# A first DFT stage moved to four 64x64 tiles of TensorE, with the mirrored sum formed ahead of it and the even and odd parts behind it

## The chip, the cores and the metric

The kernel runs on one core of a Trainium2 chip. Its time is device time in microseconds (us): the median of the runs of one kernel. The engines are TensorE (PE, with PEld for its loads of weights), VectorE (DVE), ScalarE (ACT), GpSimd (POOL) and SyncE (SP, which here only issues DMAs). Each runs its own instructions in order and waits for the others by semaphores.

## The reference

For each of 8 batches, x is 3008 x 256 in fp32. The real part of its two-dimensional Fourier transform, taken as 24064 rows of 256, goes through a feed-forward layer with the gate h * cos(h):

```python
def _attn_ref(x):                       # x: (8, 3008, 256)
    X = np.fft.fft(x, axis=1)
    X = np.fft.fft(X, axis=2)
    return X.real.astype(np.float32)

def _moe_ref(x, w_in, w_out):           # w_in: 256 x 2048, w_out: 2048 x 256
    h = x @ w_in
    g = h * np.cos(h)
    return (g @ w_out).astype(np.float32)
```

## The kernel before

**The transform.** The sequence of 3008 is split as 47 x 64. A first stage is a DFT of length 47 over rows s2 (24 of its frequencies are kept, the others follow by symmetry), a second stage one of length 64 over s1, and the DFT over the 256 columns is folded into the weights of the first feed-forward product (WC and WS). Since x is real, row s1 is joined with its mirror 64 - s1, so that 32 indices i remain, in eight chunks of four; and column d is joined with its mirror 256 - d into an even part (sum) and an odd part (difference) of 128 columns.

For one batch b and chunk c the first stage before the change does this:
- `load_x(b, p)` loads two chunks (p = 0 to 3) into an `xp` tile, the rows of x and the rows of its mirror interleaved on 96 partitions. These DMAs are issued on SP.
- `fold(b, c, e)` (L247, on GpSimd for batches 2 to 8, on VectorE for the first) forms the even part (e = 0) and the odd part (e = 1) of a chunk, 96x508; the two end columns 0 and 128 are copied by ScalarE through the list `small`.
- `first_half(b, c)` (L275) multiplies each part with its matrix from L: two matmuls of 96 rows and 64 columns of the array and 512 moving columns, the even one into partitions 0 to 63 of a PSUM bank `pz`, the odd one into 64 to 127. For chunk 0, L272 takes the first 128 columns with matrices of their own.
- `keep_z` (L301) copies `pz` to an SBUF tile `zs` on ScalarE. Column 128 is treated apart: `take_middle` gathers it into `xm`, `middle` (L323) multiplies it into `pm`, ScalarE copies that to `zm` (L917), and `patch_z` puts it into `zs`.
- `store_z` sends `zs` to DRAM (`zd`), `load_z` brings it back turned, and `second_half` (L366) is the second stage, whose result `pq` is the input of the feed-forward layer.

**The main loop.** A batch has six groups of output columns (256, the first 225) and a group has 8 steps, so `per` = 48 steps a batch; a step t has two half steps, k = 2t and 2t + 1 (u = 0, 1). For half step k, `cur`, `prev` and `old` are the units k, k - 1 and k - 2, and `done` is the step whose second product is now made. PE's order in a half step is: `mm1(cur, 0)` (L550, with WC), then second-stage matmuls `mm2(done, ...)` (L641, three of the step's seven), then `mm1(cur, 1)` (L550, with WS), and in odd half steps one `mm2` more. Around it, for each unit: `seed` (L531, ACT) writes a bias into a PSUM bank H, `act_e` (L562), `dve_h` (L566, DVE), `act_round` (L578), `dve_frac` (L582), `act_sin` (L588), `dve_g` (L592), and once a step `sums` on GpSimd (L608, L614, L615), which forms the operands S of four of the seven `mm2` matmuls. `combine_m` (GpSimd), `take_m` (ACT and DVE), `store_out` (a transpose on DVE, L761, then stores on SP) close a group.

**Where the first stage stands in it.** While batch b - 1 runs through the loop, `transform(b)` lists what is done for batch b at the end of which of the 48 steps: loads at 0, 2, 4, 6; folds of pair p at 8p + 6, 7, 9, 10; the two first-stage calls of a pair in the half step u = 0 of step 8p + 12; stores at 8p + 12; the middle column at 11. The four H banks are used in turn, and `borrow` lends the next two of them to a pair: `pz` and, with k = 1, the bank of unit k - 2, whose last reader is `dve_g`. `seed` of the next unit takes the first lent bank, so it comes behind `keep_z`.

```python
        pair = None if u else pairs.pop(t, None)
        if pair:
            b, c = pair
            pz = [first_half(b, c, borrow("pz"))]
        if old:
            dve_g(old)
            ...
        if pair:
            pz.append(first_half(b, c + 1, borrow("pz", 1)))
```

The functions in full:

Of the kernel before, what the change touches and what calls it, by code (L numbers as in the profile page):

```python
# [33 lines left out]
def _consts():  # L34
# [21 lines left out]
    LO = stack(np.sin(th), np.cos(th), -np.sin(thm), -np.cos(thm))  # L56
    LE0 = stack(np.cos(th), z, z, np.cos(thh))
    LO0 = stack(np.sin(th), z, z, np.sin(thh))
    L = np.concatenate([LE, LO, LE0, LO0], axis=1)
    L = np.concatenate([L, np.zeros((128 - NX, 256))], axis=0)  # L60

# [3 lines left out]
    for jj in range(NJ):  # L65
        phi = 2.0 * np.pi * np.outer(i, 47 * k2 + jj) / SEQ
        blk = np.concatenate([np.cos(phi), np.sin(phi)], axis=0)
        blk[0] = 1.0
        blk[NI] = np.where(k2 % 2 == 0, 1.0, -1.0)
        blk = blk.reshape(2, 2, 16, 64)  # L70
        for half in range(2):
            for r in range(2):
                for e in range(2):
                    p = 64 * half + 32 * r + 16 * e
                    B[p : p + 16, jj, 64 * e : 64 * e + 64] = blk[r, half]
# [7 lines left out]
        L.astype(np.float32),  # L83
        B.reshape(128, NJ * 128).astype(np.float32),
# [30 lines left out]
def kernel(  # L115
# [9 lines left out]
    L_np, B_np, CS_np = _consts()  # L125
    L_dr = nc.inline_tensor(L_np, name="dft_L")
    ident_dr = nc.inline_tensor(np.eye(128, dtype=np.float32), name="ident")
# [18 lines left out]
    def load_x(b, p):  # L146
        if (b, p) not in xs:
            take_x(b, p)
# [16 lines left out]

    CS = [cpool.tile([128, 256], FP, tag=f"CS{i}", name=f"CS{i}") for i in range(2)]
# [6 lines left out]
    L = cpool.tile([128, 256], FP, tag="L", name="L")  # L173
# [65 lines left out]
    def fold(b, c, e):  # L239
        lo = IP * (c % 2)  # L240
        xv = xs[b, c // 2].rearrange("r (i d) -> r i d", d=ND)[0:NX, lo : lo + IP]
        if b == 0:
            xfs[b, c] = xf0[c % 2]
        elif e == 0:
            xfs[b, c] = spool.tile([128, 2 * IP * 128], FP, tag="xf", bufs=2, name="xf")
        fv = xfs[b, c].rearrange("r (e i d) -> r e i d", e=2, d=128)[0:NX]
        (nc.gpsimd if b else nc.vector).tensor_tensor(  # L247
# [5 lines left out]
        if e:  # L253
            ends = dict(out=fv[:, :, :, 0].rearrange("r e i -> r i e"), in_=xv[:, :, 0:129:128])
            if b:
                small.append(ends)
            else:
                nc.gpsimd.tensor_copy(**ends)
# [3 lines left out]
    def first_half(b, c, pz=None):  # L262

        rows = NX if b else 128
        fv = xfs.pop((b, c)).rearrange("r (e c) -> r e c", e=2)[0:rows]
        LE, LO, LE0, LO0 = (L[0:rows, 64 * q : 64 * q + 64] for q in range(4))
        pz = pz or psum("pz", "M")
# [15 lines left out]
        if b:  # L283
            return pz
        if a:
# [5 lines left out]
            lhsT=LE,  # L291
# [4 lines left out]
        keep_z(b, c, pz)  # L296

    def keep_z(b, c, pz):
        tag, n = ("zs", 4) if b or c < 4 else ("pq", 8)
        zs = spool.tile([128, 512], FP, tag=tag, bufs=n, name="zs")  # L300
        nc.scalar.copy(out=zs, in_=pz)  # L301
        zss[b, c] = zs

    def patch_z(b, c):
        small.append(
            dict(out=zss[b, c][64:128, 0:512:128], in_=zm[64:128, IP * c : IP * c + IP])
        )

    xm = cpool.tile([128, NI], FP, tag="xm", name="xm")
    zm = cpool.tile([128, NI], FP, tag="zm", name="zm")  # L310

    def take_middle(b, p):
        xv = xs[b, p].rearrange("r (i d) -> r i d", d=ND)[0:NX]
        small.append(dict(out=xm[0:NX, XP * p : XP * p + XP], in_=xv[:, :, 128]))

    def clear_middle():
        pm = borrow("pm", 1)[64:128, 0:NI]
# [3 lines left out]
    def middle(pm):  # L321
        for i0, i1, q in ((0, 1, 2), (1, NI, 0)):
            nc.tensor.matmul(  # L323
                pm[:, i0:i1],
                lhsT=L[0:NX, 64 * q : 64 * q + 64],
                rhs=xm[0:NX, i0:i1],
                start=False,
                stop=True,
                skip_group_check=True,
# [5 lines left out]
    def store_z(b, c, j0=0, j1=NJ, eng=nc.sync):  # L335
        half, q = divmod(c, NCH // 2)
        if q == 0 and j0 == 0:
            zds[b, half] = dpool.tile([32, 2 * NJ * 128], FP, tag="zd", bufs=4, name="zd")
        zd, zs = zds[b, half], zss[b, c]
        for e in range(2):  # L340
# [4 lines left out]
            )  # L345

# [57 lines left out]
    def transform(b):  # L404
# [5 lines left out]
        for p in range(4):  # L410
            at(2 * p, load_x, b, p)
            at(7 + p, take_middle, b, p)
            for k in range(4):
                at(8 * p + (6, 7, 9, 10)[k], fold, b, 2 * p + k // 2, k % 2)
            pairs[per * (b - 1) + 8 * p + 12] = b, 2 * p
            for c in (2 * p, 2 * p + 1):
                at(8 * p + 12, store_z, b, c)
        middles.add(per * (b - 1) + 11)
# [365 lines left out]
    def chunk(c):  # L784
        fold(0, c, 0)
        fold(0, c, 1)
# [5 lines left out]
    first_half(0, 0)  # L792
    chunk(2)
    first_half(0, 1)
# [3 lines left out]
    store_z(0, 0, 0, 4)  # L798
    store_z(0, 1, 0, 4)
    chunk(3)  # L800
    first_half(0, 2)
    chunk(4)
    first_half(0, 3)
    store_z(0, 2, 0, 4)
    store_z(0, 3, 0, 4)
    chunk(5)
    first_half(0, 4)
    chunk(6)
    first_half(0, 5)
    store_z(0, 4, 0, 4, nc.scalar)  # L810
    store_z(0, 5, 0, 4, nc.scalar)
    load_z(0, 0, 0, 4)
    chunk(7)
    first_half(0, 6)
    store_z(0, 6, 0, 4, nc.scalar)
    first_half(0, 7)
# [179 lines left out]
```

## Time and profile before

| | |
|---|---|
| median of 3 runs | 1945.69 us (1945.51 to 1946.28) |
| the profiled execution | 1945.75 us, span 1944.0 us |
| granted TensorE clock | 0.999 |
| busy: PE, ACT, DVE, POOL | 99%, 78%, 75%, 72% of the span |
| share of the 16 DMA engines | 19.2% for the queue q1 over the span, 7 tenths in the first fortieth |
| first-stage matmuls L275 | 256 records, 63.1 us busy |
| folds on POOL, L247 | 112 of 1264 ns |
| copies of pz on ACT, L301 | 64 of 576 ns |

A matmul in fp32 stands in the trace as two records. A record's duration contains its way through the array, so the distance from start to start is what counts. The span starts with the first instruction; the time of an execution has 1.75 us around it. A bracket behind a line of the timeline tells how long the engine was idle before it and what ended that; for PEld this is not idle time of PE, which may still be streaming.

### The profile page before, as it was taken

What the parts mean: (1) busy time and instruction counts of PE and PEld (TensorE: products, weight loads), DVE (VectorE), ACT (ScalarE), POOL (GpSimd) and SP (SyncE); (2) the same over time, 40 slices, a digit from 0 to 9 for tenths busy, and PEclk for the clock granted to TensorE, in tenths of its full rate; (3) what the DMA queues carried; (4) which work ended last, traced back from release to release, by engine and by line L of the source; (5) the groups of instructions that cost most, each with busy time, mean ns of one, the idle gap of its engine ahead of it and who ended that gap; (6) DMA issues with size and microseconds to landing.
All of it is one profiled execution on the core that took longest, in us unless ns stands there. A gap on an engine that the chain in (4) does not pass through costs nothing.

```text
span 1944.0 us, 29626 instructions
## 1 busy us (share of the span) xinstructions
PE 1934.2 (99%) x9234; PEld 1681.9 (87%) x9234; DVE 1459.2 (75%) x2532; ACT 1508.4 (78%) x3444; POOL 1398.0 (72%) x1594
## 2 busy tenths in 40 slices
PE   9999999999999999999999999999999999999998
PEld 5888898888988889888898888988889888898887
DVE  4777777777777777777777777777777777788787
ACT  4777778777787787878778787788777887778775
POOL 3777767786677766787668776677767777666765
PEclk9999999999999999999999999999999999999999
DMA  7511122021220223111130111311013111100001
GB/s 201 129 29 39 35 53 71 18 40 40 57 58 18 42 43 80 32 24 40 40 90 21 39 25 41 88 24 40 22 42 88 24 39 28 39 23 16 11 14 31
DMA packets 178494, 89.10 MB, mean 46 GB/s; under 512 B 104945, under 2 KB 175391, under 8 KB 176674
## 3 DMA queue, kind: packets, MB, share of 16 engines
q1 hardware_dynamic: 176636, 86.68, 19.2%
q8 instruction: 75, 1.23, 0.3%
q10 hardware_dynamic: 1702, 0.53, 0.1%
q14 instruction: 81, 0.66, 0.1%
HBM read 49.90 MB, written 37.28 MB: 45 GB/s over the span
## 4 chain that ended last, share of the span: by engine, by line
PE 98%; DMA 1%; SPq 0%; DVE 0%; ACT 0%; issue 0%; POOL 0%; POOLq 0%; DVEq 0%
PE M L641 58%; PE H L550 33%; PE pz L275 3%; PE pb L366 2%; DMA wn<-wd 1%; DMA xp<-in_x_dram 1%; PE pw L433 1%; PE pz L272 0%; SPq L154 0%; PE pm L323 0%; DVE r L582 0%; ACT r L588 0%; DVE cb L709 0%; SPq L157 0%; SPq L156 0%
## 5 line engine op out<-in xcount | busy, mean ns | idle before, releaser
L608 POOL TENSOR_TENSOR S<-r 128x512 f32<-128x512 f32 (+1 forms) x383 | 475.0, 1240 | 445.5 <-DVE r L592 396.6
L582 DVE SCALAR_TENSOR_TENSOR r<-r,H 128x512 f32<-128x512 f32 (+1 forms) x768 | 518.8, 675 | 194.6 <-ACT r L578 167.9
L588 ACT ACTIVATE r<-r 128x512 f32<-128x512 f32 (+1 forms) x768 | 477.0, 621 | 240.5 <-DVE r L582 235.6
L592 DVE SCALAR_TENSOR_TENSOR r<-H,r 128x512 f32<-128x512 f32 (+1 forms) x768 | 519.1, 676 | 131.1 <-ACT r L588 90.6
L641 PE MATMUL M<-S,VX 128*128 128x256 f32 (+1 forms) x2304 | 615.2, 376 | 0.0
L641 PEld LDWEIGHTS M<-S,VX 128*128 128x128 f32 x2304 | 435.4, 190 | 71.3 <-issue 22.7
L550 PE MATMUL H<-pq,WC 128*128 128x256 f32 (+1 forms) x1536 | 453.4, 377 | 0.4 <-ACT H L531 0.3
L550 PE MATMUL H<-pq,WS 128*128 128x256 f32 (+1 forms) x1536 | 451.1, 375 | 0.5 <-ACT ew L562 0.5
L578 ACT ACTIVATE r<-H 128x512 f32<-128x512 f32 (+1 forms) x768 | 447.7, 583 | 0.2 <-DVE H L566 0.2
L566 DVE TENSOR_TENSOR H<-ew,H 128x256 f32<-128x256 f32 (+1 forms) x768 | 324.8, 423 | 140.3 <-PE H L550 81.3
L641 PE MATMUL M<-r,w 128*128 128x256 f32 (+1 forms) x1536 | 387.7, 375 | 0.0
L562 ACT ACTIVATE ew<-H 128x256 f32<-128x256 f32 (+1 forms) x768 | 287.8, 375 | 120.2 <-PE H L550 115.9
L531 ACT ACTIVATE H<-nb,wn 128x256 f32<-128x256 f32 (+1 forms) x766 | 366.0, 478 | 2.3 <-DMA wn<-wd 1.4
L641 PEld LDWEIGHTS M<-r,w 128*128 128x128 f32 x1536 | 300.4, 196 | 27.1 <-DVE mr L666 0.2
L550 PEld LDWEIGHTS H<-pq,WS 128*128 128x128 f32 x1536 | 289.9, 190 | 34.5 <-issue 1.0
L550 PEld LDWEIGHTS H<-pq,WC 128*128 128x128 f32 x1536 | 279.2, 190 | 44.6 <-ACT H L531 9.3
L614 POOL TENSOR_TENSOR S<-S,r 128x256 f32<-128x256 f32 (+1 forms) x383 | 275.5, 719 | 30.0
L615 POOL TENSOR_TENSOR S<-r,S 128x256 f32<-128x256 f32 (+1 forms) x383 | 274.5, 717 | 30.0
L641 PE MATMUL M<-S,w 128*128 128x256 f32 (+1 forms) x768 | 225.2, 375 | 0.0
L641 PE MATMUL M<-r,VX 128*128 128x256 f32 (+1 forms) x768 | 225.1, 375 | 0.0
L641 PEld LDWEIGHTS M<-S,w 128*128 128x128 f32 x768 | 150.4, 196 | 14.6
L641 PEld LDWEIGHTS M<-r,VX 128*128 128x128 f32 x768 | 145.8, 190 | 14.6
(78 smaller groups left out, 918.3 us busy)
## 6 DMA issues: line engine op xcount, KB each, us to landing
out_dram<-ob SPq DMA_DIRECT2D x724, 32.0 KB
xp<-in_x_dram SPq DMA_DIRECT2D x56, 256.0 KB
zd<-zs SPq DMA_DIRECT2D x112, 96.0 KB
z<-zd SPq DMA_DIRECT2D x28, 384.0 KB
xp<-in_x_dram SPq DMA_DIRECT2D x56, 128.0 KB
nb<-nd SPq DMA_DIRECT2D x39, 128.0 KB
wr<-in_moe_w_in_dram SPq DMA_DIRECT2D x8, 256.0 KB
w<-in_moe_w_out_dram SPq DMA_DIRECT2D x4, 512.0 KB
```

Source lines behind the costliest of these rows:

```text
L531: nc.scalar.activation(out=h.H[:, 0:T], in_=s.nb[:, 0:T], func=AF.Copy, bias=0.25, scale=wn[:, f : f + 1])
L550: nc.tensor.matmul(h.H[:, 0:T], lhsT=W[:, 128 * f : 128 * f + 128], rhs=s.pq[:, e * T : e * T + T], start=False, stop=True, skip_group_che ...
L562: nc.scalar.mul(out=h.ew[:, 0:T], in_=h.H[:, 0:T], mul=2.0)
L566: nc.vector.tensor_tensor(out=h.H[:, T : 2 * T][:, ::-1], in0=h.ew[:, 0:T], in1=h.H[:, 0:T], op=ALU.subtract)
L578: nc.scalar.activation(out=r, in_=y, func=AF.Copy, bias=BIG, scale=1.0)
L582: nc.vector.scalar_tensor_tensor(out=r, in0=r, scalar=-BIG, in1=y, op0=ALU.add, op1=ALU.subtract)
L588: nc.scalar.activation(out=r, in_=r, func=AF.Sin, bias=0.0, scale=SIN_SCALE)
L592: nc.vector.scalar_tensor_tensor(out=r, in0=y, scalar=-0.25, in1=r, op0=ALU.add, op1=ALU.mult)
L608: tt(out=sv[:, 0:2], in0=qv[:, 1:2].to_broadcast([128, 2, T]), in1=qv[:, 0:4:3], op=ALU.subtract,)
L614: tt(out=sv[:, 2], in0=sv[:, 1], in1=gv[:, 0, 0], op=ALU.subtract)
L615: tt(out=sv[:, 3], in0=gv[:, 1, 0], in1=sv[:, 2], op=ALU.add)
L641: nc.tensor.matmul(acc[key][m // 2][:, 256 * (m % 2) : 256 * (m % 2) + T], lhsT=w, rhs=a, start=first, stop=s.fp == 7, skip_group_check=True,)
```

## The change

Batch 1 keeps its way, but for signs in its matrices (a matrix LM takes over where LE stood for column 128) and the names of its functions. For batches 2 to 8 the order of the two foldings is changed. Since the first stage is linear, the even and odd parts over d can be formed behind it.

- `turn_x` copies the mirrored half of x, in reverse order of s1, from DRAM to a DRAM tile `xr`. `load_xx` then loads an `xp` tile in which partitions 0 to 46 and 64 to 110 hold four indices each (q = 0, 1), rows of x in one half of the tile and rows of the mirror, from `xr`, in the other. For p = 0 it also loads the rows of s1 = 0 and 32 into `xz`. These are 9 DMAs for p = 0 and 5 for each other p, besides the 4 of `turn_x`; before there were 6 and 4.
- `fold_x` adds the rows and their mirror in one sweep, 111x512, twice for each p (GpSimd).
- `pair_half` multiplies the sum: for q and h = 0, 1 a matmul of 47 rows and 64 columns with 512 moving columns, rows from partition 64q, result on partitions 64h, the two q in different banks. The whole pair now comes behind one `mm2` matmul, and at step 8p + 9.
- `keep_z` copies the two banks to a tile `zr` (from the `xp` buffers) and `fold_z` forms even and odd parts, 128x508 each, twice for each p (GpSimd), at steps 8p + 9 and 8p + 10.
- `take_middle` is an add on GpSimd (111x4), as is that for column 0 in `fold_x`; `fold_ends` forms two rows' even and odd parts from `xz` (111x127 each, GpSimd) at the end of steps 4 and 5. `middle` is now six matmuls, two of them of 129 and 127 columns, at step 10 instead of 11; `pm` and `zm` grow from 64x32 to 128x272.
- `store_pair` and `store_ends` are the stores, 18 a batch for 16.

The diff, cut to its core:

```diff
+    def turn_x(b, p):
+        if p == 0:
+            xrs[b] = dpool.tile([N2, 32 * ND], FP, tag="xr", bufs=2, name="xr")
+        i0 = 24 - XP * p
+        nc.sync.dma_start(
+            out=xrs[b][:, ND * i0 : ND * (i0 + XP)].rearrange("r (h c) -> h r c", h=2),
+            in_=x_r[b, ::-1, 32 + i0 : 32 + i0 + XP].rearrange("r (h s) d -> h r (s d)", h=2),
+        )
+    def load_xx(b, p):
+        take_x(b, p)
+        hi, lo = (xs[b, p][:, 1024 * q : 1024 * q + 1024].rearrange(
+            "r (h c) -> r h c", h=2) for q in range(2))
+        back = xrs[b].rearrange("r (i d) -> r i d", d=ND)
+        nc.sync.dma_start(out=xs[b, p][N2:64], in_=x_r[b, 0 : 64 - N2, 0:XP])
+        for q in range(2):
+            rows = slice(64 * q, 64 * q + N2)
+            i0 = XP * p + 2 * q
+            i1 = 27 - i0
+            ahead = x_r[b, :, i0 : i0 + 8].rearrange("r (h s) d -> r h (s d)", s=4)
+            nc.sync.dma_start(out=lo[rows], in_=ahead[:, :, 0 : 2 * ND])
+            if i0 == 0:
+                nc.sync.dma_start(
+                    out=hi[rows, 0], in_=back[:, i1 : i1 + 2].rearrange("r s d -> r (s d)")
+                )
+                nc.sync.dma_start(out=hi[rows, 1, 0:ND], in_=back[:, 31])
+                nc.sync.dma_start(out=hi[rows, 1, ND : 2 * ND], in_=x_r[b, :, 0])
+            else:
+                last = min(i1, 24)
+                at = ND * (i1 - last)
+                src = back[:, last : last + 8].rearrange("r (h s) d -> r h (s d)", s=4)
+                nc.sync.dma_start(out=hi[rows], in_=src[:, :, at : at + 2 * ND])
+        if p == 0:
+            for q in range(2):
+                nc.sync.dma_start(out=xz[64 * q : 64 * q + N2], in_=x_r[b, :, 32 * q])
...
-    def fold(b, c, e):
...
+    def ends_of(b, p, d):
+        hi, lo = (xs[b, p][0:RX, 1024 * q : 1024 * q + 1024].rearrange(
+            "r (i d) -> r i d", d=ND) for q in range(2))
+        return dict(in0=lo[:, :, d], in1=hi[:, ::-1, d], op=ALU.add)
 
     def take_middle(b, p):
-        xv = xs[b, p].rearrange("r (i d) -> r i d", d=ND)[0:NX]
-        small.append(dict(out=xm[0:NX, XP * p : XP * p + XP], in_=xv[:, :, 128]))
+        nc.gpsimd.tensor_tensor(out=xm[0:RX, 4 * p : 4 * p + 4], **ends_of(b, p, 128))
+
+    def fold_x(b, p, q):
+        if q == 0:
+            ws[b, p] = spool.tile([128, 1024], FP, tag="xf", bufs=1, name="xf")
+        xt, wt = xs[b, p][0:RX], ws[b, p][0:RX]
+        f = 512 * q
+        nc.gpsimd.tensor_tensor(
+            out=wt[:, f : f + 512],
+            in0=xt[:, 1024 + f : 1536 + f],
+            in1=xt[:, 1024 - f : 512 - f : -1],
+            op=ALU.add,
+        )
+        if q:
+            nc.gpsimd.tensor_tensor(
+                out=wt.rearrange("r (i d) -> r i d", d=ND)[:, :, 0], **ends_of(b, p, 0)
+            )
+
+    def fold_ends(e):
+        lo, hi = xz[0:RX, 1:128], xz[0:RX, 255:128:-1]
+        at = 129 if e else 1
+        nc.gpsimd.tensor_tensor(
+            out=xzf[0:RX, at : at + 127], in0=lo, in1=hi, op=ALU.subtract if e else ALU.add
+        )
+        if e:
+            small.append(dict(out=xzf[0:RX, 0:129:128], in_=xz[0:RX, 0:129:128]))
+
+    def pair_half(b, p, q, pz):
+        rows = slice(64 * q, 64 * q + N2)
+        for h in range(2):
+            nc.tensor.matmul(
+                pz[64 * h : 64 * h + 64],
+                lhsT=L2[rows, 0:64],
+                rhs=ws[b, p][rows, 512 * h : 512 * h + 512],
+                start=True,
+                stop=True,
+            )
+
+    def keep_z(b, p, q, pz):
+        if q == 0:
+            zrs[b, p] = spool.tile([128, XP * ND], FP, tag="xp", bufs=4, name="zr")
+        nc.scalar.copy(out=zrs[b, p][:, 512 * q : 512 * q + 512], in_=pz)
+
+    def fold_z(b, p, e):
+        if e == 0:
+            zfs[b, p] = spool.tile([128, 1024], FP, tag="zs", bufs=2, name="zs")
+        zr = zrs[b, p][:, 0:1024].rearrange("y (i d) -> y i d", d=ND)
+        zv = zfs[b, p].rearrange("y (e i d) -> y e i d", e=2, d=128)
+        nc.gpsimd.tensor_tensor(
+            out=zv[:, e, :, 1:128],
+            in0=zr[:, :, 1:128],
+            in1=zr[:, :, 255:128:-1],
+            op=ALU.subtract if e else ALU.add,
+        )
+
+    def patch_z(b, p):
+        zr = zrs[b, p][:, 0:1024].rearrange("y (i d) -> y i d", d=ND)
+        zv = zfs[b, p].rearrange("y (e i d) -> y e i d", e=2, d=128)
+        zq = zm[:, 0:16].rearrange("y (q p s) -> y p q s", q=2, s=2)
+        small.append(dict(out=zv[:, 0, :, 0], in_=zr[:, :, 0]))
+        small.append(dict(out=zv[:, 1, :, 0].rearrange("y (q s) -> y q s", s=2), in_=zq[:, p]))
     def clear_middle():
-        pm = borrow("pm", 1)[64:128, 0:NI]
+        pm = borrow("pm", 1)[:, 0 : 16 + ND]
         nc.vector.memset(pm, 0.0)
         return pm
 
     def middle(pm):
-        for i0, i1, q in ((0, 1, 2), (1, NI, 0)):
+        xv = xm[0:RX].rearrange("r (p h s) -> r h p s", h=2, s=2)
+        todo = [
+            (pm[64 * h : 64 * h + 64, 8 * q : 8 * q + 8], L2[0:RX, 64 + 64 * q : 128 + 64 * q], xv[:, h])
+            for q in range(2)
+            for h in range(2)
+        ]
+        todo.append((pm[0:64, 16:145], L2[0:RX, 192:256], xzf[0:RX, 0:129]))
+        todo.append((pm[0:64, 145:272], L2[0:RX, 256:320], xzf[0:RX, 129:256]))
+        for to, w, rhs in todo:
             nc.tensor.matmul(
-                pm[:, i0:i1],
-                lhsT=L[0:NX, 64 * q : 64 * q + 64],
-                rhs=xm[0:NX, i0:i1],
-                start=False,
-                stop=True,
-                skip_group_check=True,
+                to, lhsT=w, rhs=rhs, start=False, stop=True, skip_group_check=True
             )
...
         for p in range(4):
-            at(2 * p, load_x, b, p)
-            at(7 + p, take_middle, b, p)
-            for k in range(4):
-                at(8 * p + (6, 7, 9, 10)[k], fold, b, 2 * p + k // 2, k % 2)
-            pairs[per * (b - 1) + 8 * p + 12] = b, 2 * p
-            for c in (2 * p, 2 * p + 1):
-                at(8 * p + 12, store_z, b, c)
-        middles.add(per * (b - 1) + 11)
+            at(max(p - 1, 0), turn_x, b, p)
+            at(1 + p, load_xx, b, p)
+            at(5 + p, take_middle, b, p)
+            for k in range(2):
+                at(8 * p + 6 + k, fold_x, b, p, k)
+                at(8 * p + 9 + k, fold_z, b, p, k)
+            pairs[per * (b - 1) + 8 * p + 9] = b, p
+            at(8 * p + 11, patch_z, b, p)
+            at(8 * p + 12, store_pair, b, p)
+        for e in range(2):
+            at(4 + e, fold_ends, e)
+        middles.add(per * (b - 1) + 10)
+        at(12, store_ends, b)
         at(23, load_z, b, 0)
...
+    nc.sync.dma_start(out=L2, in_=L2_dr.ap())
...
         pair = None if u else pairs.pop(t, None)
-        if pair:
-            b, c = pair
-            pz = [first_half(b, c, borrow("pz"))]
         if old:
             dve_g(old)
             if old.u:
                 sums(old.s)
-        if pair:
-            pz.append(first_half(b, c + 1, borrow("pz", 1)))
         pm = clear_middle() if u and t in middles else None
         if done:
             order = (0, 1, 5, 4, 3, 2, 6) if done is steps[-1] else range(7)
-            mm2(done, 4 * v, 4 * v + 3, order)
+            mm2(done, 4 * v, 4 * v + (1 if pair else 3), order)
+        if pair:
+            pz = [borrow("pz"), borrow("pz", 1)]
+            for q in range(2):
+                pair_half(*pair, q, pz[q])
+            mm2(done, 4 * v + 1, 4 * v + 3, order)
         if pm is not None:
             middle(pm)
         if full and full is not steps[-1]:
...
         if prev:
             act_round(prev)
         if pm is not None:
-            nc.scalar.copy(out=zm[64:128], in_=pm)
+            nc.scalar.copy(out=zm, in_=pm)
         if pair:
-            keep_z(b, c, pz[0])
+            keep_z(*pair, 0, pz[0])
         if nxt and k >= AHEAD - 1:
             seed(nxt)
         if full and full is not steps[-1]:
...
         if prev:
             act_sin(prev)
         if pair:
-            keep_z(b, c + 1, pz[1])
-            patch_z(b, c)
-            patch_z(b, c + 1)
+            keep_z(*pair, 1, pz[1])
         if cur and k >= AHEAD - 1:
             mm1(cur, 1)
         if done and v == 0:
```

## The prediction

> **What bounds the kernel now.** I read the page first: busy shares, then the chain that ended last.
>
> ```profile
> span 1944.0 us, 29626 instructions
> ...
> PE 1934.2 (99%) x9234; PEld 1681.9 (87%) x9234; DVE 1459.2 (75%) x2532; ACT 1508.4 (78%) x3444; POOL 1398.0 (72%) x1594
> ...
> PE M L641 58%; PE H L550 33%; PE pz L275 3%; PE pb L366 2%; DMA wn<-wd 1%; DMA xp<-in_x_dram 1%; PE pw L433 1%; PE pz L272 0%; SPq L154 0%; PE pm L323 0%; DVE r L582 0%; ACT r L588 0%; DVE cb L709 0%; SPq L157 0%; SPq L156 0%
> ```
>
> TensorE (PE) is the chain from end to end. So only two things move the time: the PE time of the edited calls (pz, pm), and any new wait in front of PE. I therefore took the timeline around one pair of first-stage calls, and one half step without a pair.
>
> ```profile
> 370.87 0.59 PE L550 MATMUL H<-pq,WC 128*128 128x256 f32 x2
> ...
> 371.31 0.69 DVE L592 SCALAR_TENSOR_TENSOR r<-H,r 128x512 f32<-128x512 f32 x1 [0.25 <-ACT r L588]
> ...
> 371.39 1.94 PE L275 MATMUL pz<-xf,L 96*64 96x512 f32 x8
> ...
> 372.06 0.39 PEld L275 LDWEIGHTS pz<-xf,L 96*64 96x64 f32 x4 [0.47 <-DVE r L592]
> ...
> 372.52 0.59 ACT L301 COPY zs<-pz 128x512 f32<-128x512 f32 x1
> ...
> 373.13 0.48 ACT L531 ACTIVATE H<-nb,wn 128x256 f32<-128x256 f32 x1
> ...
> 373.26 1.13 PE L641 MATMUL M<-S,VX 128*128 128x256 f32 x4
> ...
> 375.09 0.59 PE L550 MATMUL H<-pq,WC 128*128 128x256 f32 x2
> ```
>
> ```profile
> 382.43 0.59 PE L550 MATMUL H<-pq,WC 128*128 128x256 f32 x2
> 382.86 1.03 PE L641 MATMUL M<-S,VX 128*128 128x256 f32 x4
> ...
> 384.59 0.59 PE L550 MATMUL H<-pq,WC 128*128 128x256 f32 x2
> ```
>
> Each fp32 matmul is two records. A plain one of 256 columns takes 0.43 us from start to start (382.43 to 382.86), one record 0.215; a record of 512 columns is twice that, 0.43. From WC to WC an even half step takes 2.16 us without a pair and 4.22 with one: a pair costs 2.06 us. Its eight records would stream 3.43 us one after another; they fit because the two column halves (e = 0, 1) run side by side: 4 x 0.43 = 1.71, and the other 0.35 goes into changing the array's tiling (0.09 from 371.30 to 371.39, the rest behind).
>
> **The pair, after.** It is still four matmuls of 512 columns (q, h = 0, 1), but each on its own 64x64 tile, and the two q write different banks. If all four run side by side they stream 2 x 0.43 = 0.86, plus the same 0.35. What is in the way is the bank of q = 1: it is that of unit k-2 and is read last by L592. In the rows above the second load of weights waited for L592 until 372.06, but PE was streaming until then, so it cost nothing. Now one second-stage matmul stands ahead of the pair (0.43): q = 0 can start at 371.30 + 0.43 + 0.09 = 371.82, q = 1 at 372.06 in that place. The pair moves from steps 12, 20, 28, 36 of a batch to 9, 17, 25, 33, where the trace has L592 ending 0.59 us after WC's columns are in (0.70 in the rows above) for the last three, and 0.80 for the first, whose covering matmul has 225 columns (0.375). With 0.06 from L592's end to the load:
> - last three: wait 0.59 + 0.06 - 0.43 - 0.09 = 0.13. Cost 0.35 + 0.86 + 0.13 = 1.34, a gain of 0.72;
> - first: wait 0.80 + 0.06 - 0.375 - 0.09 = 0.39. Cost 1.60, a gain of 0.46.
> Seven batches: 21 x 0.72 + 7 x 0.46 = **18.3 us gained**. No trace here shows four tiles at once; the bounds are 28 x 0.86 = 24 (all beside, wait covered) and 0 (row halves in turn). I take the upper mechanism, since the nearest row, the column halves, start within 10 ns of each other.
>
> **The middle column (pm).**
>
> ```profile
> 329.48 0.42 PE L323 MATMUL pm<-xm,L 96*64 96x1 f32 x4
> 329.83 0.30 PEld L550 LDWEIGHTS H<-pq,WS 128*128 128x128 f32 x2
> ...
> 562.16 0.69 DVE L592 SCALAR_TENSOR_TENSOR r<-H,r 128x512 f32<-128x512 f32 x1 [0.35 <-ACT r L588]
> ...
> 562.58 0.59 PE L550 MATMUL H<-pq,WS 128*128 128x256 f32 x2
> ```
>
> Now: four small records 0.06 apart, 0.55 us in all on PE. After: eight small records and four of 127 to 129 columns in one column half (4 x 0.108 = 0.43), at step 10 instead of 11. There PE is ready at 562.58, but L592 ends at 562.85 and behind it the memset now clears 128x272 of PSUM (0.29 by the 246 ns of L868's 128x225, against 85 ns), so pm starts near 563.2. That is 0.6 wait + 0.46 + 0.43 + 0.25 change = 1.75, **1.2 more, 8.4 us over seven batches**. Bounds: 0.65 each (4.6 in all) if the small ones overlap by column halves and L592 comes as early as at step 11; 1.5 each (10.5) if the longer copy of pm on ACT (128x272, about 0.4 for 0.18) also delays L531.
>
> **The start of batch 2.** This is the wait that the change adds. GpSimd (POOL) runs in order, and at the end of step 4 it now has fold_ends, which needs xz; xz is issued last of nine loads of load_xx(1, 0), three of which wait on SP for turn_x's DRAM copy. Behind fold_ends on POOL queue L608, L614, L615 of the next step, whose result PE needs.
>
> ```profile
> 1.45 6.06 PE L497 MATMUL pd<-VX 128*128 128x512 f32 x8 [1.45 <-DVE VX L488]
> ...
> 60.36 1.05 POOL L608 TENSOR_TENSOR S<-r 128x450 f32<-128x450 f32 x1
> ...
> 61.13 0.51 SPq L156 DMA_DIRECT2D xp<-in_x_dram  x1
> ...
> 65.55 0.54 PE L641 MATMUL M<-S,VX 128*128 128x225 f32 x2
> ```
>
> Before, SP's second x load went out only at 61.13, behind the weights and BJ, whose packets keep the DMA engines over 90% busy from 46 to 58. After: turn_x(1, 0) goes out near 61.1 and lands some 3.3 later (loads issued at 62.35 and 63.00 landed in 2.4 to 2.9); from 64.5 seven issues at 0.62 put the last xz out at 68.2 to 68.9, landing near 70.3. fold_ends is 0.46 (198 ns + 2.04 ns a column, by 1240 ns for L608's 512 columns and 719 for L614's 256), so L608 ends at about 72.0 instead of 61.41. PE needs it at 65.55, so 4.14 is cover: **PE waits some 6.5 us, once**. Bounds: 3.7 if SP isn't held to 61.1 and xz lands at 67.5; 9.1 if the idle PE also loses its clock, priced by the opening row, where eight 512-column records took 6.06 us for 3.43 of streaming, 2.6 lost. (The Trainium skill, "TensorE: Matmul & The Clock Gate", part 1, has the clock halved after an idle window of about 3.4 us; by it 9.1 is the likelier end and the sum would be 2.6 higher. The trace agrees as far as it goes: after PE's last matmul near 1938.5 the granted clock is 0.90 in 1940 to 1942 and 0.50 in 1942 to 1944.)
>
> In batches 3 to 8 the same loads come in time: at batch 4, SP would issue the turns at 760.3, the eight out stores from 763.5 to 768.2, load_xx's nine to 773.8, landed by 776.3; POOL reaches fold_ends behind the sums of 774.8, at 777.5.
>
> **Edits at about nothing.** POOL keeps 16 large folds a batch at L247's 1264 ns; it gains two of 0.46 and eight tiny strided adds (0.21 by the slope above, 0.68 if like L258's 96x8 copy): 2.6 to 6.4 us a batch, in steps 4 to 8, under those 3.5 to 4 us by which each step's sums end before PE wants them; bare, it would cost PE what exceeds that. ACT loses three 0.2 us copies a quarter batch. SP gets 12 issues more a batch (7 us of its idle time). DVE's other work and batch 1 are unchanged.
>
> **Sum**, against the profiled execution of 1945.75 us (0.06 above the median): -18.3 + 8.4 + 6.5 = -3.4, so **1942 us**, a hair from the 0.2% (3.9 us) that a measurement of this kernel can tell from no change.
>
> **Rivals.**
> 1. *Row halves take turns* (slower). Two q on the same PSUM partitions run one behind the other: the pair costs 2.06 again, nothing is gained, the other terms stay: 1945.7 + 8.4 + 6.5 = 1960.6. It decides as soon as a pair costs over about 1.53 us (gain below 14.9 in all). For: no row shows two row tiles. Against: column halves overlap fully.
> 2. *Evacuation sets the pace* (also slower). Both banks are still emptied by two copies of 0.58 (L301), with L531 between, and the next WC must wait for L531. In the new order q = 0 is streamed at 372.7, its copy starts at 372.9 and L531 ends at 374.0; PE wants WC at about 374.4. That clears by 0.3 us; if ACT is later by 0.3 to 0.6, 28 pairs lose 8 to 17 us: 1950 to 1959, which outdoes the gain from 0.15 us a pair on. For: take_m's copies follow in the very next step; against: ACT is 78% busy. (The Trainium skill, "TensorEngine Tiling (Array Packing)", PSUM Bottleneck, warns of this: tiling speeds up PE, not the emptying of PSUM. In the trace the copies are not yet on the chain.)
> 3. *All covered.* L592 comes earlier beside a shorter pair and batch 2 starts with little wait: -22 + 5 + 3.7 = -13, 1932.
>
> **Chances.** Forecast 0.50 (own range 1936 to 1949), rival 1 0.12, rival 2 0.16, rival 3 0.22. Faster: all of rival 3 and half of the forecast, 0.47; within 0.2%: most of the forecast's other half, 0.26; the rest 0.27. The range runs from 1929 (all covered, with every low bound) to 1954, leaving out rival 1 and the worst of rival 2.
>
> **What would show it.** Right: pz records of 47 rows, four starts within some 20 ns or the second two 0.1 to 0.4 later on L592; WC to WC 3.4 to 3.7 us in pair halves; pm near 1.7; one PE gap of 4 to 9 us at 65 to 75 with POOL waiting on a DMA into xz. Wrong: q = 1 starting only when q = 0 is through; PE idle on ACT L531 after pairs; PE gaps at steps 4 to 8 of later batches.

## The result, and the profile after

The change makes the kernel slower by half: 2973.84 us (2971.99 to 2975.73) against 1945.68 us (1945.51 to 1946.29), a ratio of 1.528, 95% interval 1.526 to 1.530. The forecast was 1942 us. The profiled execution took 2974.77 us, with a span of 2973.0. These are the lines of its page that answer to those of before: the span, the busy times, and the chain that ended last, by engine and by line.

```profile
span 2973.0 us, 29786 instructions
...
PE 1994.3 (67%) x9262; PEld 1727.5 (58%) x9262; DVE 1461.9 (49%) x2532; ACT 1499.2 (50%) x3367; POOL 1413.9 (48%) x1665
...
PE 53%; SPq 36%; DMA 8%; DVE 1%; issue 1%; ACT 0%; POOL 0%; DVEq 0%; POOLq 0%
PE M L785 32%; PE H L694 18%; SPq L215 13%; SPq L204 7%; DMA xp<-xr 5%; SPq L198 4%; SPq L923 3%; SPq L218 3%; SPq L187 2%; SPq L206 2%; PE pb L505 1%; DMA xp<-in_x_dram 1%; SPq L210 1%; SPq L209 1%; PE pz L396 1%
```

Every engine has about the work that was expected: POOL is busy 16 us longer, DVE and ACT are within 10 us of before. But PE, which was 91% of the chain by its two main lines alone, is now 53% in all, and 36% is SPq: SP's own queue, standing in the DMA issues of load_xx (L198 to L218) and turn_x (L187). PE itself is idle for 979 us of the span, against 10 before, and busy for 60 us longer; together that is 1029 us, the whole loss. The edited PE work is not the cause. This is the timeline of an undisturbed pair (columns: start, duration, engine, line):

```profile
1468.00 0.59 PE L694 MATMUL H<-pq,WC 128*128 128x256 f32 x2
...
1468.95 1.19 PE L396 MATMUL pz<-xf,L 47*64 47x512 f32 x8
...
1470.69 0.48 ACT L675 ACTIVATE H<-nb,wn 128x256 f32<-128x256 f32 x1
...
1471.47 0.38 PE L694 MATMUL H<-pq,WC 128*128 128x256 f32 x1
```

WC to WC is 3.47 us where a half step without a pair takes 2.16: the pair costs 1.31, as against 2.06 before and 1.34 in the prediction. What went wrong is in the waits (engine, line, what it waited for: us in all, times, longest):

```profile
POOL xm L366 <- DMA xp<-xr: 740.4, 21, 39.1
...
PE M L785 <- POOL S L752: 458.5, 14, 33.5
...
POOL xzf L387 <- DMA xz<-in_x_dram: 332.9, 7, 57.0
...
ACT xzf L286 <- DMA xz<-in_x_dram: 309.6, 7, 54.4
...
PE H L694 <- ACT ew L706: 303.8, 8, 53.5
...
PE pm L443 <- POOL xm L366: 199.3, 7, 28.8
```

GpSimd stands 740 us in take_middle and 333 in fold_ends, 28 waits, four for each of the seven batches. ScalarE waits too: fold_ends leaves it a copy of two columns out of xz (L286, the list `small`), and it stands there for 310 us. So PE is held up in three places, for 962 us in all. At step 6 of a batch it waits for `ew` from ScalarE, whose own work stands behind that small copy (304 us). At steps 8 and 9 it waits for the sums S from GpSimd (459 us), and at step 10 for `xm`, from which it makes the middle column (199 us). One of the waits for S on the timeline:

```profile
1284.31 0.59 PE L694 MATMUL H<-pq,WS 128*128 128x256 f32 x2
...
1297.83 9.18 SPq L187 DMA_DIRECT2D xr<-in_x_dram  x1
...
1312.91 8.09 SPq L215 DMA_DIRECT2D xp<-xr  x1
1316.29 0.20 POOL L366 TENSOR_TENSOR xm<-xp 111x4 f32<-111x4 f32 x1 [34.27 <-DMA xp<-xr]
1316.44 1.06 POOL L752 TENSOR_TENSOR S<-r 128x450 f32<-128x450 f32 x1
1317.55 1.12 PE L785 MATMUL M<-S,VX 128*128 128x225 f32 x2 [32.65 <-POOL S L752]
```

Read it upwards from the end: PE waits 32.65 us for the sum S; S stands on POOL behind a 0.2 us add of four columns; that add waits 34.27 us for its load; and SP needs 8 to 9 us for each of the two issues shown, where an issue took 0.62 in the kernel before. The transfers themselves show why. The columns of the windows are: stretch, its length, busy time of PE, PEld, DVE, ACT and POOL, granted clock, share of the 16 DMA engines, GB/s.

```profile
63.00:71.00 8.00, 3.51 (x18) 3.09 (x17) 1.22 (x3) 1.43 (x4) 0.00 (x0) 0.90 0.12 50
472.00:484.00 12.00, 0.00 (x0) 0.00 (x0) 0.00 (x0) 0.00 (x0) 0.00 (x0) 0.50 0.07 24
484.00:496.00 12.00, 0.00 (x0) 0.00 (x0) 0.00 (x0) 0.00 (x0) 0.00 (x0) 0.50 0.07 25
```

From 472 to 496 us no engine does anything, only loads of x are under way, and the DMA share is 0.07: one engine of sixteen (0.0625), at 24 to 25 GB/s. While turn_x copies (63 to 71) it is 0.12, two of sixteen, at 50 GB/s. In 472 to 496 the granted clock is 0.50 as well, which fits the 60 us by which PE is busy longer for the same kind of work.

**Theory A**, formed from these windows: a DMA is spread over as many engines as the largest number up to 16 that divides its outermost size. load_xx's DMAs have 47 rows, or 17: both prime and over 16, so one engine. turn_x's copy has h = 2 outermost: two engines. The loads of before had 32 and 16 rows. (The Trainium skill, "DMA: Bandwidth & Descriptors", paragraph "How many engines (k)", states this rule for the slowest dimension longer than 1 of both access patterns, with 127 partitions on one engine among its examples; the DMA shares of 0.07 and 0.12 agree with it, and the runs below test it.) The amounts fit: by the view of DMA issues a batch moves 3646 KB in DMAs of 47 or 17 rows (in all 56 x 188, 28 x 136 and 21 x 47 from x, 49 x 188, 7 x 94 and 7 x 47 from xr) and 1504 KB in copies. At 24.5 and 50 GB/s these take 152 + 31 = 183 us, and the loads of one batch were seen in flight from 442 to 629, 187 us. In the kernel before, by the starts of WC, 34 to 37 us pass between the end of step 0, where the copies start, and the end of step 8, where the last load is first used. By this estimate some 146 to 149 us a batch aren't covered; 147 a batch are lost.

**Rivals.** B: it is the change's order that costs, with DMAs behind DRAM copies on SP and folds ahead of the sums on GpSimd, whatever the rows. C: it is turn_x's copies alone. D: what helps in a version with split loads is smaller DMAs or more of them, not their engines. E: what is then left against before is order. Below, a stretch is the 48 steps of the loop in which one batch is prepared; some of the expectations call it a quarter.

### The profile page after: what moved, and what is told of

Read it like the earlier page. It is cut to its first block, busy times and chain, and to the rows that moved or that the text cites. A ratio compares the mean times of both kernels' runs of the same rounds, so it can differ in the third digit from the quotient of the medians.

```text
span 2973.0 us, 29786 instructions
## 1 busy us (share of the span) xinstructions
PE 1994.3 (67%) x9262; PEld 1727.5 (58%) x9262; DVE 1461.9 (49%) x2532; ACT 1499.2 (50%) x3367; POOL 1413.9 (48%) x1665
## 4 chain that ended last, share of the span: by engine, by line
PE 53%; SPq 36%; DMA 8%; DVE 1%; issue 1%; ACT 0%; POOL 0%; DVEq 0%; POOLq 0%
PE M L785 32%; PE H L694 18%; SPq L215 13%; SPq L204 7%; DMA xp<-xr 5%; SPq L198 4%; SPq L923 3%; SPq L218 3%; SPq L187 2%; SPq L206 2%; PE pb L505 1%; DMA xp<-in_x_dram 1%; SPq L210 1%; SPq L209 1%; PE pz L396 1%
## 5 line engine op out<-in xcount | busy, mean ns | idle before, releaser
L785 PE MATMUL M<-S,VX 128*128 128x256 f32 (+1 forms) x2304 | 651.6, 391 | 458.5 <-POOL S L752 458.5
L785 PEld LDWEIGHTS M<-S,VX 128*128 128x128 f32 x2304 | 453.7, 199 | 546.5 <-POOL S L752 464.1
L694 PE MATMUL H<-pq,WS 128*128 128x256 f32 (+1 forms) x1536 | 464.5, 385 | 303.8 <-ACT ew L706 303.8
L694 PEld LDWEIGHTS H<-pq,WS 128*128 128x128 f32 x1536 | 297.1, 195 | 343.6 <-ACT ew L706 306.4
L694 PE MATMUL H<-pq,WC 128*128 128x256 f32 (+1 forms) x1536 | 466.8, 386 | 0.1
L675 ACT ACTIVATE H<-nb,wn 128x256 f32<-128x256 f32 (+1 forms) x766 | 366.2, 478 | 0.9
L694 PEld LDWEIGHTS H<-pq,WC 128*128 128x128 f32 x1536 | 292.2, 197 | 45.0 <-ACT H L675 5.2
L785 PE MATMUL M<-S,w 128*128 128x256 f32 (+1 forms) x768 | 232.1, 385 | 0.0
L905 DVE STREAM_TRANSPOSE ob<-cb 128x512 f32<-128x512 f32 x94 | 67.0, 713 | 208.3 <-POOL cb L840 206.2
```

Of the source, the lines that this page charges most:

```text
L675: nc.scalar.activation(out=h.H[:, 0:T], in_=s.nb[:, 0:T], func=AF.Copy, bias=0.25, scale=wn[:, f : f + 1])
L694: nc.tensor.matmul(h.H[:, 0:T], lhsT=W[:, 128 * f : 128 * f + 128], rhs=s.pq[:, e * T : e * T + T], start=False, stop=True, skip_group_che ...
L785: nc.tensor.matmul(acc[key][m // 2][:, 256 * (m % 2) : 256 * (m % 2) + T], lhsT=w, rhs=a, start=first, stop=s.fp == 7, skip_group_check=True,)
```

## The experiments

**e1_split32: all DMAs of x in parts that divide well.** Order, steps and computation stay.

```
+        parts = ((0, 32), (32, 47))
+        rows_in(((0, 16), (16, 17)), xs[b, p][N2:64], ...)      # the fill
-            nc.sync.dma_start(out=lo[rows], in_=ahead[...])
+            rows_in(parts, lo[rows], ahead[...])                # and so for every load
 turn_x:
-            out=...rearrange("r (h c) -> h r c", h=2),
+            out=...rearrange("r (s d) -> s r d", d=ND),         # 8 rows outermost
```

> The changed kernel, with each load of 47 rows made as one of 32 and one of 15 rows, the fill of 17 rows as 16 and 1, and turn_x's copy with its eight s1 rows as outermost dimension instead of two halves. Same bytes, same places, about twice the loads to issue. Theory A (a DMA whose outermost dimension is 47, a prime, runs on one of the 16 DMA engines, one of 2 on two: the trace has 25 and 53 GB/s and a DMA share of 0.07 and 0.12 while they run): the loads take a tenth of the time, no wait over 20 us is left, the pair, pm and start terms of the prediction remain: 1952 us, 1938 to 1965. Theory B (it is the order: loads that wait for DRAM copies and GpSimd adds that stand at fixed steps, whatever the DMAs' width): more issues on SP, 2950 or more. Theory C (the DRAM copy of turn_x alone is too slow): like A here.

Measured: 1964.60 us, ratio 1.0089 (1.0072 to 1.0106). Of the 1028 us lost, 1009 are gone with the outermost sizes of these DMAs alone. B is out; C expected the same here as A, and is decided by the next three runs. What is left, by half steps (starts of WC in this kernel less those in before): 12.0 us in the stretch that prepares batch 2, and 0.1 to 2.0 in each later one.

**e2_split46: the loads cut 46 + 1 rows** (`parts = ((0, 46), (46, 47))`), the fill and the copies as in the change. Each load is two DMAs as in e1, but 46 rows divide by 2 at most.

> The changed kernel, with each load of 47 rows made as one of 46 rows (2 x 23) and one of 1. As many loads as with 32 + 15; only the divisor differs; turn_x is left as it is. Theory A: 46 rows run on two engines, about 50 GB/s, so the chain of loads of a batch (187 us in the trace, 442 to 629, of which some 30 are the copies of turn_x) falls to about 105; GpSimd wants the last of them about 40 us after the first, so 65 us a batch are lost for 147: 2350 to 2500 us. Theory B: 2950 or more. Theory C: 2950.

Measured, in one run: 2536.03 us, 36 over the top of what A gave, 414 under what B and C gave. While the engines wait for such loads, the DMA share is that of two engines of sixteen (0.125), at 46 GB/s:

```profile
468.00:481.00 13.00, 0.00 (x0) 0.00 (x0) 0.00 (x0) 0.00 (x0) 0.00 (x0) 0.59 0.13 46
```

The number of DMAs is not what counts, since e4, below, has as many loads and the same copies: it is the divisor. With the copies on two engines throughout, the time is 2974 with loads on one engine, 2536 on two, and 2087 with 32 and 15 rows (e4).

**e3_before29: the kernel before, with nothing changed but rows.** In batches 2 to 8 its loads of 32 rows go as 29 + 3 and those of 16 as 13 + 3.

> The kernel before, in which only the loads of x for batches 2 to 8 are cut otherwise: rows 0 to 28 and 29 to 31 instead of 0 to 31, rows 31 to 43 and 44 to 46 instead of 31 to 46. 29 and 13 are primes. No copy in DRAM, no new order. Theory A: 84 of 96 rows of a tile run on one engine at about 25 GB/s, 27 us for a quarter of a batch, some 115 us for all; the last quarter is wanted by ScalarE's copy of the middle column at step 10, some 48 us after the first load, so 55 to 70 us a batch are lost: 2300 to 2450 us. Theories B and C: nothing of theirs is in this kernel, 1946 to 1955.

Measured, in one run: 2342.51 us, in A's range. The kernel before, with its own order and without any copy, loses 396 us when its main loads have 29 rows; B and C had nothing to lose here. That the range held is in part luck: 13 is a prime but under 16, so by A's own rule the loads of 13 rows run on thirteen engines, and 58 of the 96 rows, not 84, on one. The trace bears this out: the first loads of three parts go out at 375.3, 396.2 and 417.7 us, 21 us apart and not the 27 expected. Its chain:

```profile
PE M L645 43%; PE H L554 25%; DMA xp<-in_x_dram 20%; PE pz L279 2%; SPq L158 2%; PE pb L370 2%; DMA wn<-wd 0%; PE pw L437 0%; SPq L165 0%; ACT r L592 0%; DMA out_dram<-ob 0%; POOL S L612 0%; ACT r L582 0%; DVE r L586 0%; SPq L783 0%
```

A fifth of it is DMA into xp, which had 1% before. This is the plainest proof that neither four tiles nor mirrored sums are needed for such a loss.

**e4_loads32: e1 with turn_x's copy left on two engines.**

> The changed kernel with the loads cut into 32 + 15 rows as in the first run, but turn_x's copy left on two engines (53 GB/s, 7 us for a quarter). Theory A: the copies' 28 us a batch mostly lie ahead of their use, 1955 to 2030 us. Theory B: 2950 or more. Theory C: still over 2700, as the copy is what is waited for.

Measured, in one run: 2087.08 us, 57 above A's range and far under B's and C's: against before the stretch that prepares batch 2 loses 27 us and each later one 18 to 19, mostly at steps 6 and 9. GpSimd's longest wait is this; ScalarE waits 72 us for the same xz, and PE 66 us behind it:

```profile
POOL xzf L389 <- DMA xz<-in_x_dram: 96.7, 7, 23.2
```

xz isn't turned at all; it is issued behind the loads that wait for the copy, on the same in-order queue. A's estimate had left that out. So the single engine of the loads makes the larger part of the loss, and the copies on two engines a smaller one.

**e6_rows48: 48 rows instead of 47.** The row ahead of the batch's first comes along and meets a zero weight; the fill is 16 rows, the copies have 8 rows outermost. One DMA a load, one small copy more a batch (it puts the row ahead into xr), and the steps as in the change.

```
-        rows = slice(64 * q, 64 * q + N2)
+        rows = slice(64 * q + 1, 64 * q + 48)     # in L2; row 64 * q stays zero
+        own = x_b[N2 * b - 1 : N2 * b + N2]       # x_b: x with (b s2) as one row index
-            rows = slice(64 * q, 64 * q + N2)     # in the loads and pair_half
+            rows = slice(64 * q, 64 * q + 48)
```

> The kernel after with 48 rows in each load of x instead of 47: the row in front of the batch's first comes along, with a zero weight in L2; the fill is 16 rows; turn_x's copy has the eight s1 rows outermost. One DMA for each load as in the kernel after (29 issues a batch, against 50 in e1_split32), same steps of the plan. Theory A (a load is spread over the largest number of engines up to 16 that divides its outermost size; 47 gives one, 48 gives sixteen): the stalls are gone as in e1_split32, and with about half the issues SP is ahead of it: the start of batch 2 falls from 11.9 to about 7 to 9 us, the middle column from 2.9 to 1.5 to 2.5 us a batch; 1950 us, between 1942 and 1962. Rival D (what e1 gained comes from smaller packets or more DMAs in flight, not from the number of engines of each DMA): with as few DMAs as in the kernel after it stays above 2500. Rival E (what is left in e1 against the kernel before has nothing to do with the number of issues, but with order): 1962 to 1967, as e1.

Measured: 1946.57 us, ratio 1.0001 (0.9991 to 1.0010), in A's range, and D and E are out: 29 DMAs of x a batch, for 28 in the change and 52 in e1, take away even the lateness in the later stretches. Whether the fewer issues do that, or sixteen engines where e1 has loads of 15 rows, the run doesn't tell. By half steps each later stretch is now 1.3 to 1.6 us *shorter* than before, and the one that prepares batch 2 costs 9.1. This is the change with its transfers as the prediction had supposed them, and so the place to read its other terms. The middle column in its timeline:

```profile
809.92 0.28 DVE L440 MEMSET pm<- 128x272 f32 x1
...
810.35 0.41 PE L453 MATMUL pm<-xm,L 112*64 112x8 f32 x8 [0.67 <-DVE pm L440]
...
810.58 0.63 PE L453 MATMUL pm<-xzf,L 112*64 112x129 f32 x4
```

**e7_xzfirst: e1 with xz loaded ahead of the other loads.**

> e1_split32 with one thing moved: the two column blocks of xz are loaded ahead of all of the next batch's other loads (in step 0 of its quarter, not behind load_xx of part 0). If the start of batch 2 waits for xz behind the copy turn_x on SP's queue, as the prediction had it, GpSimd's wait in fold_ends (20.8 us in e1, 14.1 of it at batch 2) falls below 8 and the kernel gains 3 to 9 us on e1: 1955 to 1962. If what holds it is take_middle and fold_x behind the loads of part 0 all the same, it gains under 2 us: 1963 to 1966.

Measured: 1960.96 us, ratio 1.0074 (1.0060 to 1.0087): 3.6 under e1, in the range of the first theory, but the intervals of the two overlap, and the reason is not its own. fold_ends no longer waits for xz at the start; GpSimd then stands in take_middle for 7.7 us instead, and the stretch costs 12.3 us, no less than e1's 12.0. What the profiled run gains on e1 is in the later stretches.

**e5_best: e6 with the plan moved.**

```
-            at(max(p - 1, 0), turn_x, b, p)
-            at(1 + p, load_xx, b, p)
-            at(5 + p, take_middle, b, p)
+            at(0, turn_x, b, p)
+            at(1, load_xx, b, p)
+            at(6 + p, take_middle, b, p)
+        at(0, load_xz, b)                         # behind the copies
-            at(4 + e, fold_ends, e)
+            at(5 + 3 * e, fold_ends, e)
-        middles.add(per * (b - 1) + 10)
+        middles.add(per * (b - 1) + 11)
```

> e6_rows48 with the plan's steps changed: all four turn_x and the loads of xz at step 0 of a quarter, load_xx at step 1, take_middle one step later (6 + p), fold_ends at steps 5 and 8, the middle column at step 11 and not 10. Nothing of the computation changes. By theory A with the terms as measured in e1 (pairs: three of 0.75 and one of about 0.2 to 0.46 a batch, 17 to 19 us in all; middle column 0.9 to 1.3 a batch, 6 to 9 us, once GpSimd is not late; start of batch 2 some 2 to 5 us): 1945.7 - 18 + 7.5 + 3.5 = 1938, between 1932 and 1947: faster than before by 0 to 0.7%. If GpSimd's lateness in steps 5 to 8 isn't due to loads, the middle column stays near 2.9 and it ends at 1948 to 1958. Rival D: above 2500.

Measured: 1940.34 us, ratio 0.9973 (0.9962 to 0.9984): faster than before by 0.3%, in its range. Later stretches gain 1.6 to 1.9 us each; the start still costs 6.4 (4.5 in its stretch, which holds a gain of 1.9 too), above the 2 to 5 expected. The second call of fold_ends, and with it ScalarE's copy out of xz, now comes at step 8: at the start PE waits 3.7 us for S from GpSimd, and no longer behind ScalarE as in e6 (7.8).

**e8_xzahead and e9_inturn: the start.** e8 is e5 with load_xz ahead of the copies:

> e5_best with one thing moved: the two loads of xz go out ahead of the four turn_x copies of the same step, not behind them. In e5 the start of batch 2 costs 6.4 us between the starts of WC of steps 7 and 9; its chain stands on xz, issued at 64.1 to 66.5 and landed at 72.3, with GpSimd 7.3 us in fold_ends and TensorE 4.1 us on the S behind it. Theory (the prediction's own for the start: fold_ends in front of the sums waits for xz): xz lands near 65, GpSimd does not wait, the 4.1 us go, and with them part of the lost clock behind them; nothing else changes: 1934 to 1937. Rival: the loads of part 0, which go out 0.5 us later or no earlier, hold take_middle and fold_x instead, and the gain is under 2 us: 1938.5 to 1940.5.

Measured: 1943.07 us, ratio 0.9978 (0.9968 to 0.9987), not to be told from e5 and outside both ranges. In the profiled runs the start costs 10.0 us, against 6.4 in e5: fold_ends doesn't wait any more, take_middle does, and PE waits 6.2 us for S. e9 is e8 with only one copy ahead of the loads of part 0 (`at(p, turn_x, b, p)`, `at(1 + p, load_xx, b, p)`):

> e8_xzahead with the other edit of e5 undone: turn_x of part p goes out at step p and load_xx of part p at step 1 + p, so that between xz and the loads of part 0 only one DRAM copy stands on SP's queue and not four. In e8 the wait of batch 2's start moved from fold_ends to take_middle (8.7 us on the loads of part 0 behind the four copies). Theory (the start is one queue: whichever transfer stands behind the copies is waited for): the loads of part 0 land near 70, GpSimd's wait falls below 3 us, the start costs 0 to 3 us: 1933 to 1938. Rival (the first quarter's DMA engines are full whatever the order: weights, BJ, x of batch 2): the wait stays above 6 us, 1940 to 1944. In batches 3 to 8 both expect -1.6 to -1.9 a batch as in e5.

Measured: 1938.21 us, ratio 0.9957 (0.9943 to 0.9970), 0.2 over its range and the lowest median of all (its interval overlaps that of e5). GpSimd's timeline at the start of batch 2 in e6, e8 and e9, the idle time and its releaser in brackets:

```profile
73.31 0.45 POOL L397 TENSOR_TENSOR xzf<-xz 112x127 f32<-112x127 f32 x1 [12.14 <-DMA xz<-in_x_dram]
```

```profile
77.82 0.20 POOL L374 TENSOR_TENSOR xm<-xp 112x4 f32<-112x4 f32 x1 [8.74 <-DMA xp<-xr]
```

```profile
72.79 0.21 POOL L374 TENSOR_TENSOR xm<-xp 112x4 f32<-112x4 f32 x1 [2.03 <-DMA xp<-in_x_dram]
```

The wait goes to whatever stands behind the copies on SP: xz in e6, the loads of part 0 in e8. In e9, where one copy stands ahead of the first piece needed and not four, it falls to 2.0 us, under the 3 expected; for the next two parts GpSimd waits 1.8 and 4.4 us more. PE's long wait at the start is gone; it waits 1.3 us ahead of the first pair and 1.5 for S at 89 us. The start still costs 4.6 us (2.7 in its stretch and the gain of 1.9), over the 0 to 3 expected.

## Why the prediction was wrong

**The step that failed** is the sentence "In batches 3 to 8 the same loads come in time", with "landed by 776.3", and the price under it: an issue of 0.62 us and a landing in 2.4 to 2.9, taken from loads of 32 and 16 rows and put on loads of 47 rows and on a copy with two blocks outermost. The prediction counted DMAs ("12 issues more a batch") and never asked over how many engines one of them runs; no bound was set for a shape that the trace did not hold. Measured: 24 to 25 GB/s on one engine, 187 us a batch, issues of 4.5 to 14.9 us for the loads out of xr (L215), and 147 us a batch on the end, the whole miss. None of the three rivals held it either: all of them had the loads in time. The prediction's sign of being wrong, PE gaps at steps 4 to 8 of later batches, came in part: the gaps are at steps 6, 8, 9 and 10.

**The pair: right.** By half steps, e6 has 3.48 against 2.16 without a pair: 1.32, predicted 1.34. The first pair of a batch costs 1.57 (3.58 less 2.01), predicted 1.60. So 0.74 and 0.49 gained, 19.0 us in all against 18.3 predicted, but for the first pair of batch 2, which waits. In the pair shown above the first four of the eight records start at 0, 0.006, 0.117 and 0.124 us: row halves do run side by side, and the second q comes 0.12 later, predicted 0.13. Rival 1 (halves in turn) is out.

**Evacuation (rival 2): out.** In the pair shown above L675 is through at 1471.17 and WC starts at 1471.47: the margin of 0.3 us that the prediction worked out. In e6, with all 28 pairs, PE is nowhere idle for 0.3 us or more ahead of WC.

**The middle column: right once loads come in time.** In e6 the half step takes 4.34 us against 2.61, so 1.73, and 0.06 later; predicted 1.75. Before it was 0.64 (predicted 0.55): 1.15 more, predicted 1.2. Moved to step 11 in e5 it is 1.40, some 0.3 less. In e1, where GpSimd is late, the same half step grows by 2.9 to 3.2 instead of 1.7: the price held only under the cover of loads in time.

**The start of batch 2: the right transfer, but half of the path missed, and too small.** fold_ends does wait for xz behind the copies, and the sums behind it. But in e6 it is not S that PE waits for, it is `ew` from ScalarE, which stands in its own copy out of xz. This is ScalarE's wait in e6, and PE's line on the timeline:

```profile
ACT xzf L296 <- DMA xz<-in_x_dram: 8.7, 1, 8.7
```

```profile
74.23 1.12 PE L704 MATMUL H<-pq,WS 128*128 128x225 f32 x2 [7.78 <-ACT ew L716]
```

The prediction counted ScalarE's copies only as fewer, not that a new one waits for xz. The way through GpSimd ends at about the same time (its first sum is through at 74.78), so without this copy PE would, by this row, still have waited for S. Predicted 6.5 with bounds 3.7 to 9.1; in e6 GpSimd gets xz at 73.3 (predicted 70.3), and the start costs 10.7 (9.1, and the 1.6 gained in its stretch), above the upper bound. PE waits 7.8, then runs its first records at half pace (1.12 us for two of 225 columns, 0.54 in full clock), and the first pair waits another 1.5. It was taken too low at how long the copies hold the queue, and at the lost clock, which was kept for the upper bound. (That bound was also what the rule in the Trainium skill, "TensorE: Matmul & The Clock Gate", part 1, pointed to, half clock behind an idle stretch; the rows here agree: 0.50 in the idle windows of the change, and the half pace just named.) The row that priced the lost clock at 2.6 doesn't show it, though: the view of windows gives that stretch, 1 to 8 us in the kernel before, a granted clock of 1.00. In e6 it is 0.50 for 3 us, so some 1.5 us are lost to it.

**Edits at about nothing: right in their sizes.** The tiny adds take 0.21 us, fold_ends 0.45, the memset 0.285, as estimated. But a small step that waits for a load is not at nothing: what stands behind it in its engine's order waits too. With the transfers mended the forecast of 1942 stands beside 1946.6 (e6); 4.2 of the 4.6 us between them is the start. The profiled execution of e6 also opens 1.4 us later than that of before; e8 and e9, whose code up to there is the same, open only 0.1 later, so this differs between executions, and why stays open.

## What to carry to other kernels

Before a DMA is priced by another one's row, compare the outermost sizes of both access patterns: here loads of 32, 48 or 16 rows came fast enough, 47 rows ran at the DMA share of one engine, and a copy ordered as two blocks at that of two. In this kernel a useless row (48 for 47, with a zero weight) is cheaper than an exact load or a split one. And where engines run in order, ask of each new consumer what stands behind it: here an add of 0.2 us on GpSimd held up the sums, and so the array, for 33 us at a time, and a copy of two columns on ScalarE held it up for 41 to 54 us.

## What the runs showed of the hardware that was not expected

- DMAs of 47 rows move 24 to 25 GB/s with a DMA share of 0.07; those of 46 rows 46 GB/s with 0.13; a copy with two blocks outermost 50 GB/s with 0.12.
- When such DMAs pile up, the issue itself gets slow: the 49 loads out of xr at L215 take 4.5 to 14.9 us on SP, half of them over 7.7; in e6, with 48 rows, they take 0.3 to 1.0. SP's queue then is 36% of the chain, with the stores of the output behind it too.
- Four 64x64 tiles in fp32 stream eight records of 512 columns in about 1.0 us (an estimate: the eighth starts 0.60 behind the first, and a record takes 0.43), and with the change of tiling a pair costs 1.32 on the path (e6).
- The clock that PE loses in a wait is paid again behind it. These are the windows of e6 at the start of batch 2, in the wait, in the 3 us behind it, and in the next 3:

```profile
66.00:73.50 7.50, 0.45 (x3) 0.10 (x1) 0.00 (x0) 0.24 (x2) 0.19 (x1) 0.79 0.82 226
74.00:77.00 3.00, 2.77 (x7) 2.47 (x8) 2.24 (x4) 1.65 (x5) 2.84 (x5) 0.50 1.05 186
77.00:80.00 3.00, 3.00 (x17) 2.97 (x16) 1.74 (x4) 2.58 (x7) 2.90 (x5) 0.97 1.07 183
```

The granted clock is 0.50 for about 3 us of work, and 7 records of PE fit where the next 3 us hold 17. The transfers that are waited for run at a DMA share of 0.82 and 226 GB/s here: the same kind of loads as in the idle windows of the change, and copies, now with 48 rows and with 8 blocks outermost.
